# Weight rounding with two buffers per intermediate, a fourth staging place in two accumulators, and small softmax operations on POOL

## The chip, the cores and the metric

The kernel runs on one core of a Trainium2 chip. The time is the device time of one execution in microseconds; the median of three runs is 748.48 us (747.7 to 748.65). A core has five engines that work side by side and wait for one another by semaphores: TensorE (PE in the profile) multiplies matrices into PSUM, VectorE (DVE) and ScalarE (ACT) work on tiles in PSUM and SBUF, GpSimd (POOL) on tiles in SBUF alone, and SyncE (SP) issues the DMA transfers here. Each engine executes its own queue in order.

## The reference

Attention in both directions between 512 tokens and 32 state rows per head (4 batches, 8 heads, 64 features), then two pairs of dense layers over the 2176 resulting rows: 512 to 2048 with a leaky activation and back, and 512 to 2048 with softplus and back.

```
a = softmax(0.125 * x @ state^T);   xread = a @ state
a2 = softmax(0.125 * state @ x^T);  sread = a2 @ x
x = concat(xread, sread) per batch, heads side by side   # (2176, 512)
h = x @ w_in;  g = max(h, 0) + alpha * min(h, 0);  x = g @ w_out
h = x @ w2_in; g = max(h, 0) + log1p(exp(-abs(h)));  out = g @ w2_out
```

The weights come as 64-bit floats; x, state and the output are 32-bit.

## The kernel before

The work is cut into blocks of 512 columns: q counts the four quarters of the 2048 hidden features, b the four batches of 512 tokens, and b = 4 is a block of the 4 x 32 state rows. A matrix product is made of three matmuls (`mm3`, lines 140 to 142), because each operand is held as a high part and a low part of the remainder (`split`, lines 146 and 149).

**Weights.** There are 64 weight tiles of 128 x 512 64-bit numbers. Tile i is loaded by SP into one of three staging tiles `stg` (`wload`, line 192). `wconv` turns it into 32-bit numbers: ACT takes the exponent field from the top 16 bits into `exp` (L206) and rescales it into `top` (L207), DVE puts in the sign (L208), cuts out the exponent (L209) and multiplies the low 32 bits by it (L210), and POOL adds both parts (L211). There is one `top` and one `exp` tile. The result goes into its final place for the first layer's input weights (`is_whole`, tiles wi0h to wi3l), otherwise into one of four `cnv` tiles, from which `wprep` splits it into a high part (ACT) and a low part (POOL). `wconv` returns without work when it is as many tiles ahead of `wprep` as there are `cnv` tiles. At its end it calls `wload` for the next tile.

**Attention.** Eight groups i (a batch and one half of its heads) go through four steps: `at_scores` (s: scores on PE L273, copy on ACT L274, row maximum on DVE L275, L276 scales it, exponential on ACT L277, L278 adds a small number to the sum, reciprocal L279), `at_rows` (r: transposes L287, the softmax the other way, L290 to L296), `at_back` (b: transposes L303 and a split) and `at_read` (d: transposes L312, products L318, L328). Loads x (at_load_t, L254) and y (at_load_x, L258) bring a group's two forms of the tokens; y is first read in L318, x in L273. The scratch tiles of a group are taken from places that later hold accumulators or weights.

**State weights.** `sw_batch` (w, PE L242) multiplies the state of one batch by four whole weight tiles; block (q, b) of the first layer needs its result.

**Order.** The program text gives an order: the string LOADS (L is `wload`), then BEFORE, then the blocks, between the first of which the strings AMONG are called. In it p is `wprep` and c is `wconv`. The framework then sets the order of each engine's queue by a planned timeline of its own (`schedule_with_timeline_sim=True`), so that an instruction whose inputs the plan sees ready may pass earlier ones of the text; queues in the trace differ from the text accordingly. A block is `hidden` (PE, into one of four PSUM banks `pa`), `act` (ACT, DVE) and, three blocks later, `out_part` (PE, four banks `pb`), whose sums `out_take` gathers in the 17 accumulators acc0 to acc16.

Of the kernel before, what the change touches and what calls it, by code (L numbers as in the profile page):

```python
# [8 lines left out]
F32 = mybir.dt.float32  # L9
F32R = mybir.dt.float32r  # L10
BF16 = mybir.dt.bfloat16
U16 = mybir.dt.uint16
U32 = mybir.dt.uint32
I64 = mybir.dt.int64
AF = mybir.ActivationFunctionType
ALU = mybir.AluOpType
AX = mybir.AxisListType

P = 128
W = 512  # L20
# [5 lines left out]
SCALE = 0.125  # L26
# [16 lines left out]

LOADS = "L0 x0 L0 y0 x1 L0 x2 y2 y1"
BEFORE = "p0 s0 c0 s1 r0 p0 c0 r1 d0 b0 p0 x3 d1 y3 p0 w0 b1 p0 y4 s2 p0 r2 c0 x4 s3 w1 c0"
AMONG = ("d2 r3 b2", "d3 s4 x5", "b3", "r4", "s5 y5 p0 d4 x6", "p0 r5 s6", "y6 d5 r6 b4 b5", "", "y7 x7 s7 d6", "b6 r7", "d7 b7")

# [9 lines left out]
def mixer_kernel(  # L59
# [18 lines left out]
    def sbt(shape, dt, name):  # L78
        return sb.tile(shape, dt, tag=name, name=name)
# [6 lines left out]
    class Place:  # L86


        def __init__(self, name):
            self.name, self.t, self.dt = name, None, None  # L90
# [6 lines left out]
        f = property(lambda self: self.get(F32))  # L97
        r = property(lambda self: self.get(F32R))

    def sbp(name):  # L100
        return Place(name + "h"), Place(name + "l")

# [17 lines left out]
    stf = ex_p[0][0]  # L120
    wo_p = pairs(7, "wo")
    g_p = pairs(4, "g")
    acc = [Place(f"acc{i}") for i in range(17)]
    stg = [sbt([P, W], I64, f"stg{i}") for i in range(3)]
    cnv = [sbt([P, W], F32, f"cnv{i}") for i in range(4)]
    tmp = [sbt([P, W], F32, f"tmp{i}") for i in range(3)]
    top_t = [[sbt([P, W], BF16, f"{x}{i}") for i in range(1)] for x in ("top", "exp")]
    top_bias = sbt([P, 1], F32, "top_bias")
    ident = sbt([P, P], F32, "ident")
    alpha = sbt([P, DFF // P], F32, "alpha")  # L130
# [2 lines left out]
    st_n = [sbt([P, 2], F32, f"stn{i}") for i in range(3)]  # L133


    for x in acc + flat([sr] + wo_p + g_p + wi_p[:4] + at_p + sw_p + wi_p[4:] + ex_p):
        x.get(F32)

    def mm3(ps, lh, ll, rh, rl, start, stop):
# [45 lines left out]
    def is_whole(i):  # L185
        return wsrc[i][:2] == ("i", 0)

    def wload():
        i = nload[0]
        if i < len(wsrc):  # L190
            to, of = stg[i % len(stg)].bitcast(U16), wsrc[i][4].bitcast(U16)
            nc.sync.dma_start(out=to[:, 0 : 4 * W - 1], in_=of[:, 1 : 4 * W])
            nload[0] += 1

    def wconv():

        i = nconv[0]
        if i >= len(wsrc) or i >= nprep[0] + len(cnv):
            return
        s = stg[i % len(stg)]  # L200
        top = s.bitcast(U16).rearrange("p (n t) -> p n t", t=4)[:, :, 2]
        low = s.bitcast(U32).rearrange("p (n t) -> p n t", t=2)[:, :, 0]
        a = take_place(i).f if is_whole(i) else cnv[i % len(cnv)]
        t, e = (x[i % len(x)] for x in top_t)
        tu, eu = t.bitcast(U16), e.bitcast(U16)
        nc.scalar.activation(e, top.bitcast(BF16), AF.Abs)  # L206
        nc.scalar.activation(tu, eu, AF.Relu, bias=top_bias, scale=TOP_SCALE)  # L207
        nc.vector.scalar_tensor_tensor(out=tu, in0=top, scalar=TOP_SIGN, in1=tu, op0=ALU.bitwise_and, op1=ALU.bitwise_or)  # L208
        nc.vector.tensor_scalar(eu, tu, TOP_EXP, None, op0=ALU.bitwise_and)  # L209
        nc.vector.scalar_tensor_tensor(out=a, in0=low, scalar=REST, in1=e, op0=ALU.mult, op1=ALU.mult)  # L210
        nc.gpsimd.tensor_tensor(out=a, in0=t, in1=a, op=ALU.add)  # L211
        wload()
        nconv[0] += 1

    def wprep(n=1):
# [49 lines left out]
    def at_scores(i):  # L265

        b, g = i // 2, i % 2
        t, n2 = scratch(i), st_n[i % 3]
        ps = bank(pool_s(i))
        for k in range(2):  # L270
            for hh in range(2):
                r, o = slice(hh * D, (hh + 1) * D), col(g, k, hh)
                nc.tensor.matmul(ps[o : o + NS], stf.f[r, head(2 * g + k, b)], t[k][r], start=True, stop=True)  # L273
        nc.scalar.activation(t[4], ps, AF.Copy)  # L274
        nc.vector.tensor_reduce(out=n2[:, 0:1], in_=ps, op=ALU.max, axis=AX.X)  # L275
        nc.vector.tensor_scalar(n2[:, 0:1], n2[:, 0:1], -SCALE, None, op0=ALU.mult)  # L276
        nc.scalar.activation(t[5], ps, AF.Exp, bias=n2[:, 0:1], scale=SCALE, accum_out=n2[:, 1:2])  # L277
        nc.vector.tensor_scalar(n2[:, 1:2], n2[:, 1:2], EPS, None, op0=ALU.add)  # L278
        nc.vector.reciprocal(n2[:, 1:2], n2[:, 1:2])  # L279

    def at_rows(i):

        s0, e1 = scratch(i)[4], scratch(i)[1]
        m1, s1 = st_m[i % 2], st_s[i % 2]
        ps = bank(pool_s(i))
        for c in range(4):
            nc.tensor.transpose(ps[:, c * P : (c + 1) * P], s0[:, c * P : (c + 1) * P], ident)  # L287
        p3 = ps.rearrange("p (a n) -> p a n", n=NS)
        e3 = e1.rearrange("p (a n) -> p a n", n=NS)
        nc.vector.tensor_reduce(out=m1, in_=p3, op=ALU.max, axis=AX.X)  # L290
        nc.vector.tensor_tensor(out=e3, in0=p3, in1=m1.to_broadcast([P, 16, NS]), op=ALU.subtract)
        nc.scalar.activation(e1, e1, AF.Exp, scale=SCALE)
        nc.vector.tensor_reduce(out=s1, in_=e3, op=ALU.add, axis=AX.X)
        nc.vector.tensor_scalar(s1, s1, EPS, None, op0=ALU.add)
        nc.vector.reciprocal(s1, s1)
        nc.gpsimd.tensor_tensor(out=e3, in0=e3, in1=s1.to_broadcast([P, 16, NS]), op=ALU.mult)  # L296

# [260 lines left out]
```

## Time and profile before

| | |
|---|---|
| median of the runs | 748.48 us (747.7, 748.48, 748.65) |
| the profiled execution | 746.91 us, span 745.1 us |
| mean granted TensorE clock | 0.995 of full |
| busy, share of the span | PE 97%, DVE 57%, ACT 57%, POOL 23% |
| the chain that ended last, by engine | PE 95%, DVE 2%, ACT 1%, DMA 1% |
| DMA | 47.27 MB, mean 63 GB/s |

The profile is of one execution, whose own time stands beside its span: the 1.8 us between them lie outside the program's own instructions. Busy shares are means over stages that differ much: the first 40 us are loading, conversion and attention, the rest is mostly matmuls. A `<-` behind an idle time names what ended it. A line number names a line of the kernel before.

### The profile page before, as it was taken

Reading aid. Unit: us, or ns where it says so; the run is one execution under the profiler, and the core shown is the slowest. Engines: PE = TensorE matmul, PEld = TensorE weight load, DVE = VectorE, ACT = ScalarE, POOL = GpSimd, SP = SyncE. Lnnn points to the kernel's source line nnn. Section 1 sums busy time; section 2 is a strip of 40 time slices with the busy share of each in tenths; the row PEclk is TensorE's granted clock in tenths of the full one; section 3 lists DMA queues with packets and bytes.
Section 4 is the critical chain, followed back from the end, with each engine's and each line's share of the span. In section 5 each row is a group of like instructions: output and inputs, shape, how many; then the busy total and the mean of one; then the engine's idle time right before and its main releaser. Section 6 shows DMA issues by size and latency. Waiting matters only on the chain.

```text
span 745.1 us, 9504 instructions
## 1 busy us (share of the span) xinstructions
PE 722.4 (97%) x3580; PEld 561.6 (75%) x3580; DVE 425.2 (57%) x693; ACT 423.5 (57%) x764; POOL 170.8 (23%) x142
## 2 busy tenths in 40 slices
PE   5699998999999999999999999999999999999997
PEld 2267666777778777878888888888888888888886
DVE  4898657757778456886585224664257342333433
ACT  4778767735564235564677647765466454444560
POOL 2353332412142003462572004410044000000000
PEclk9989999999999999999999999999999999999999
DMA  9654313203211001220123001220010000001102
GB/s 320 224 177 154 104 41 128 86 1 113 85 57 57 0 1 49 93 85 1 40 74 113 0 1 45 97 86 0 1 53 5 1 1 0 1 1 56 57 15 113
DMA packets 16654, 47.27 MB, mean 63 GB/s; under 512 B 2016, under 2 KB 2016, under 8 KB 16608
## 3 DMA queue, kind: packets, MB, share of 16 engines
q1 hardware_dynamic: 16608, 46.66, 18.7%
q8 instruction: 28, 0.46, 0.3%
q14 instruction: 18, 0.15, 0.1%
HBM read 42.20 MB, written 4.46 MB: 63 GB/s over the span
## 4 chain that ended last, share of the span: by engine, by line
PE 95%; DVE 2%; ACT 1%; DMA 1%; issue 0%; POOL 0%; SPq 0%; ACTq 0%
PE pb L140 17%; PE pb L141 17%; PE pb L142 17%; PE pa L140 13%; PE pa L142 12%; PE pa L141 12%; PE pa L242 2%; PE pa L363 2%; PE pa L273 1%; DMA acc<-xt 1%; DVE top L208 1%; PE pa L371 0%; PE pa L312 0%; PE pb L273 0%; ACT exp L206 0%
## 5 line engine op out<-in xcount | busy, mean ns | idle before, releaser
L390 DVE SCALAR_TENSOR_TENSOR pa<-pa,tmp 128x512 f32<-128x512 f32 x68 | 47.4, 697 | 125.7 <-ACT tmp L389 125.7
L387 ACT ACTIVATE tmp<-pa 128x512 f32<-128x512 f32 x68 | 40.6, 597 | 89.2 <-PE pa L142 69.7
L433 DVE TENSOR_TENSOR acc<-pb,acc 128x512 f32<-128x512 f32 x102 | 67.4, 685 | 35.9 <-PE pb L142 35.9
L208 DVE SCALAR_TENSOR_TENSOR top<-stg,top 128x512 uint16<-128x512 uint16 x64 | 53.0, 828 | 47.5 <-ACT top L207 46.9
L211 POOL TENSOR_TENSOR cnv<-top,cnv 128x512 f32<-128x512 bf16 x48 | 56.3, 1174 | 100.6 <-DVE cnv L210 96.8
L383 DVE SCALAR_TENSOR_TENSOR pa<-tmp,rest,pa 128x512 f32<-128x512 f32 (+1 forms) x80 | 53.2, 671 | 25.5 <-ACT tmp L379 25.0
L206 ACT ACTIVATE exp<-stg 128x512 bf16<-128x512 bf16 x64 | 43.0, 672 | 39.6 <-DVE cnv L210 28.9
L379 ACT ACTIVATE tmp<-pa 128x512 f32<-128x512 f32 x68 | 40.2, 597 | 42.2 <-PE pa L142 35.7
L207 ACT ACTIVATE top<-exp,top_bias 128x512 uint16<-128x512 uint16 x64 | 46.2, 722 | 9.3 <-POOL cnv L211 5.7
L389 ACT ACTIVATE tmp<-tmp 128x512 f32<-128x512 f32 x68 | 42.9, 631 | 1.7
L388 ACT ACTIVATE tmp<-tmp 128x512 f32<-128x512 f32 x68 | 42.9, 631 | 1.5
L210 DVE SCALAR_TENSOR_TENSOR cnv<-stg,exp 128x512 f32<-128x512 uint32 x48 | 35.8, 745 | 12.8 <-POOL wo5l L149 4.0
L209 DVE TENSOR_SCALAR exp<-top 128x512 uint16<-128x512 uint16 x64 | 32.2, 503 | 1.1
L146 ACT ACTIVATE g1h<-pa 128x512 fp32r<-128x512 f32 x33 | 19.7, 597 | 20.5 <-DVE pa L390 12.3
L146 ACT ACTIVATE g3h<-pa 128x512 fp32r<-128x512 f32 x33 | 19.7, 597 | 19.4 <-DVE pa L383 9.7
L146 ACT ACTIVATE g0h<-pa 128x512 fp32r<-128x512 f32 x33 | 19.7, 596 | 19.1 <-DVE pa L383 10.2
L149 DVE TENSOR_TENSOR g3l<-pa,g3h 128x512 fp32r<-128x512 f32 x33 | 22.7, 689 | 13.5 <-ACT g3h L146 13.2
L149 DVE TENSOR_TENSOR g1l<-pa,g1h 128x512 fp32r<-128x512 f32 x33 | 22.7, 687 | 12.6 <-ACT g1h L146 12.2
L149 DVE TENSOR_TENSOR g0l<-pa,g0h 128x512 fp32r<-128x512 f32 x33 | 22.7, 688 | 10.5 <-ACT g0h L146 10.1
L149 DVE TENSOR_TENSOR g2l<-pa,g2h 128x512 fp32r<-128x512 f32 x33 | 22.7, 686 | 10.0 <-ACT g2h L146 9.9
L146 ACT ACTIVATE g2h<-pa 128x512 fp32r<-128x512 f32 x33 | 19.8, 599 | 14.5 <-DVE pa L390 7.6
L149 POOL TENSOR_TENSOR wo3l<-cnv,wo3h 128x512 fp32r<-128x512 f32 x5 | 6.5, 1304 | 74.5 <-ACT wo3h L146 74.3
(863 smaller groups left out, 2114.5 us busy)
## 6 DMA issues: line engine op xcount, KB each, us to landing
stg<-w1i SPq DMA_DIRECT2D x16, 511.8 KB, 4.1
stg<-w1o SPq DMA_DIRECT2D x16, 511.8 KB, 3.4
stg<-w2i SPq DMA_DIRECT2D x16, 511.8 KB, 4.0
stg<-w2o SPq DMA_DIRECT2D x16, 511.8 KB, 3.3
out<-acc SPq DMA_DIRECT2D x16, 256.0 KB, 2.0
acc<-xt SPq DMA_DIRECT2D x10, 256.0 KB, 4.5
acc<-xs SPq DMA_DIRECT2D x8, 256.0 KB, 5.1
wo4h<-xt SPq DMA_DIRECT2D x3, 256.0 KB, 3.8
```

Source lines behind the costliest of these rows:

```text
L140: nc.tensor.matmul(ps, lh, rh, start=start, stop=False)
L141: nc.tensor.matmul(ps, lh, rl, start=False, stop=False)
L142: nc.tensor.matmul(ps, ll, rh, start=False, stop=stop)
L146: nc.scalar.activation(h, src, AF.Copy)
L149: eng_l.tensor_tensor(out=l, in0=src, in1=h, op=ALU.subtract)
L206: nc.scalar.activation(e, top.bitcast(BF16), AF.Abs)
L207: nc.scalar.activation(tu, eu, AF.Relu, bias=top_bias, scale=TOP_SCALE)
L208: nc.vector.scalar_tensor_tensor(out=tu, in0=top, scalar=TOP_SIGN, in1=tu, op0=ALU.bitwise_and, op1=ALU.bitwise_or)
L211: nc.gpsimd.tensor_tensor(out=a, in0=t, in1=a, op=ALU.add)
L383: nc.vector.scalar_tensor_tensor(out=ps[:, cs], in0=t[:, cs], scalar=a, in1=ps[:, cs], op0=ALU.mult, op1=ALU.add)
L390: nc.vector.scalar_tensor_tensor(out=ps, in0=ps, scalar=0.0, in1=t, op0=ALU.max, op1=ALU.add)
L433: nc.vector.tensor_tensor(out=a, in0=ps, in1=a, op=ALU.add)
```

## The change

`top` and `exp` have two tiles each, used in turn. Of the four `cnv` tiles three remain. The accumulators acc0 and acc1 become the halves of one tile of twice the width; before they are used, the same memory is a fourth staging tile, for weight tile 3 alone, so LOADS issues four weight loads ahead of any conversion, and the conversion of tile 3 calls no `wload`. LOADS has another order: x1 and the third and fourth weights stand before y0. Three small operations of the softmax (128 x 1 twice, 128 x 16 once, per group) go from DVE to POOL.

```diff
-LOADS = "L0 x0 L0 y0 x1 L0 x2 y2 y1"
+LOADS = "L0 x0 L0 x1 L0 L0 y0 x2 y2 y1"
...
+    class Half:
+        def __init__(self, both, k):
+            self.name, self.both, self.k = f"{both['name']}{k}", both, k
+
+        @property
+        def f(self):
+            if "f" not in self.both:
+                self.both["f"] = sbt([P, 2 * W], F32, self.both["name"])
+            return self.both["f"][:, self.k * W : (self.k + 1) * W]
...
-    acc = [Place(f"acc{i}") for i in range(17)]
+    acc01 = {"name": "acc01"}
+    acc = [Half(acc01, 0), Half(acc01, 1)] + [Place(f"acc{i}") for i in range(2, 17)]
     stg = [sbt([P, W], I64, f"stg{i}") for i in range(3)]
-    cnv = [sbt([P, W], F32, f"cnv{i}") for i in range(4)]
+    stg_3 = sbt([P, W], I64, acc01["name"])
+    cnv = [sbt([P, W], F32, f"cnv{i}") for i in range(3)]
     tmp = [sbt([P, W], F32, f"tmp{i}") for i in range(3)]
-    top_t = [[sbt([P, W], BF16, f"{x}{i}") for i in range(1)] for x in ("top", "exp")]
+    top_t = [[sbt([P, W], BF16, f"{x}{i}") for i in range(2)] for x in ("top", "exp")]
...
-    for x in acc + flat([sr] + wo_p + g_p + wi_p[:4] + at_p + sw_p + wi_p[4:] + ex_p):
+    for x in acc[2:] + flat([sr] + wo_p + g_p + wi_p[:4] + at_p + sw_p + wi_p[4:] + ex_p):
...
+    def stage(i):
+        return stg_3 if i == 3 else stg[(i - (i > 3)) % len(stg)]
+
     def wload():
...
-            to, of = stg[i % len(stg)].bitcast(U16), wsrc[i][4].bitcast(U16)
+            to, of = stage(i).bitcast(U16), wsrc[i][4].bitcast(U16)
...
     def wconv():
...
-        s = stg[i % len(stg)]
+        s = stage(i)
...
-        wload()
+        if i != 3:
+            wload()
...
     def at_scores(i):
...
-        nc.vector.tensor_scalar(n2[:, 0:1], n2[:, 0:1], -SCALE, None, op0=ALU.mult)
+        nc.gpsimd.tensor_scalar(n2[:, 0:1], n2[:, 0:1], -SCALE, None, op0=ALU.mult)
         nc.scalar.activation(t[5], ps, AF.Exp, bias=n2[:, 0:1], scale=SCALE, accum_out=n2[:, 1:2])
-        nc.vector.tensor_scalar(n2[:, 1:2], n2[:, 1:2], EPS, None, op0=ALU.add)
+        nc.gpsimd.tensor_scalar(n2[:, 1:2], n2[:, 1:2], EPS, None, op0=ALU.add)
         nc.vector.reciprocal(n2[:, 1:2], n2[:, 1:2])
...
     def at_rows(i):
...
-        nc.vector.tensor_scalar(s1, s1, EPS, None, op0=ALU.add)
+        nc.gpsimd.tensor_scalar(s1, s1, EPS, None, op0=ALU.add)
         nc.vector.reciprocal(s1, s1)
```

## Rows read from the trace of the kernel before

**Rows 1.** The page: busy time and share of the span, TensorE

```profile
PE 722.4 (97%) x3580; PEld 561.6 (75%) x3580; DVE 425.2 (57%) x693; ACT 423.5 (57%) x764; POOL 170.8 (23%) x142
```

**Rows 2.** Stages: window, its length, busy time of each engine, clock, DMA share, GB/s

```profile
7.00:14.00 7.00, 6.01 (x19) 1.96 (x20) 4.88 (x12) 3.98 (x8) 1.16 (x1) 1.00 1.03 393
...
21.00:28.00 7.00, 5.51 (x63) 1.93 (x64) 4.37 (x10) 4.43 (x12) 2.27 (x3) 1.00 0.84 297
28.00:34.70 6.70, 3.44 (x28) 1.36 (x27) 6.23 (x14) 5.12 (x13) 2.43 (x2) 1.00 0.39 130
34.70:41.50 6.80, 6.09 (x50) 3.73 (x50) 6.68 (x15) 5.40 (x11) 3.90 (x3) 0.50 0.33 98
41.50:50.00 8.50, 8.50 (x78) 4.88 (x75) 8.43 (x17) 8.15 (x21) 4.99 (x4) 1.00 0.79 258
...
122.00:741.00 619.00, 619.00 (x2824) 498.17 (x2823) 334.72 (x511) 336.74 (x576) 129.85 (x102) 1.00 0.13 43
```

**Rows 3.** The list of waits of TensorE: total us, times, longest

```profile
PE pa L140 <- DVE g1l L149: 2.4, 1, 2.4
PE pa L312 <- ACT at7l L277: 1.9, 1, 1.9
...
PE pa L242 <- POOL wi1l L211: 1.4, 1, 1.4
```

**Rows 4.** Timeline of TensorE: start, duration, instruction, idle before it and its releaser

```profile
7.20 2.49 PE L273 MATMUL pb<-acc,ex0h 64*32 64x512 f32 x8 [7.20 <-DMA acc<-xt]
...
16.66 0.65 PE L318 MATMUL pa<-acc,acc 128*32 128x64 f32 x32
...
35.41 0.79 PE L140 MATMUL pa<-at0h,sw0h 128*128 128x512 f32 x1 [1.40 <-DVE stn L276]
```

**Rows 5.** The chain that ended last, 7 to 60 us: start, us

```profile
36.20 0.43 PE pa L141
...
42.28 0.23 PE pa L141
```

**Rows 6.** Timeline of ACT, 24 to 27 us

```profile
24.70 0.66 ACT L206 ACTIVATE exp<-stg 128x512 bf16<-128x512 bf16 x1 [1.56 <-DVE wi1l L210]
25.94 0.72 ACT L207 ACTIVATE top<-exp,top_bias 128x512 uint16<-128x512 uint16 x1 [0.58 <-POOL wi1l L211]
```

**Rows 7.** Timeline of DVE, 15 to 36 us

```profile
15.12 0.17 DVE L294 TENSOR_SCALAR sts<-sts 128x16 f32<-128x16 f32 x1
15.32 0.25 DVE L295 RECIPROCAL sts<-sts 128x16 f32<-128x16 f32 x1
...
16.78 0.15 DVE L276 TENSOR_SCALAR stn<-stn 128x1 f32<-128x1 f32 x1
16.86 0.68 DVE L290 TENSOR_REDUCE stm<-pa 128x16 f32<-128x512 f32 x1
...
21.85 1.29 DVE L208 SCALAR_TENSOR_TENSOR top<-stg,top 128x512 uint16<-128x512 uint16 x1 [0.47 <-ACT top L207]
...
26.70 0.69 DVE L208 SCALAR_TENSOR_TENSOR top<-stg,top 128x512 uint16<-128x512 uint16 x1 [2.03 <-ACT top L207]
27.42 0.29 DVE L209 TENSOR_SCALAR exp<-top 128x512 uint16<-128x512 uint16 x1
```

**Rows 8.** Timeline of POOL

```profile
21.55 1.05 POOL L296 TENSOR_TENSOR wo4l<-wo4l,sts 128x512 f32<-128x512 f32 x1 [0.49 <-DVE sts L295]
...
71.24 1.17 POOL L211 TENSOR_TENSOR wi3l<-top,wi3l 128x512 f32<-128x512 bf16 x1 [2.17 <-DVE wi3l L210]
```

**Rows 9.** DVE's groups by line, 7 to 60 us: busy, mean ns, idle before

```profile
L208 DVE SCALAR_TENSOR_TENSOR top<-stg,top 128x512 uint16<-128x512 uint16 x10 | 9.3, 934 | 9.8 <-ACT top L207 9.8
L209 DVE TENSOR_SCALAR exp<-top 128x512 uint16<-128x512 uint16 x10 | 4.6, 459 | 0.2
```

**Rows 10.** Timeline of SP's queue

```profile
13.27 0.33 SPq L192 DMA_DIRECT2D stg<-w1i  x1
```

**Rows 11.** The chain that ended last, whole span

```profile
104.47 1.02 PE pa L242 x16
```

## The prediction, made before the result was known

> **What bounds the kernel now.** I read the page's engine line first: TensorE is busy 722.4 us, 97% [rows 1]. The table by stage says where the other 3% lies: from 122 to 741 us TensorE is busy 619.00 of 619.00 us, so nothing that shortens another engine there can shorten the kernel; from 28 to 34.7 us it is busy 3.44 of 6.70 [rows 2]. The list of waits gives the pieces: 1.4 us until POOL finished the fourth rounded weight (wi1l), 1.9 us until ACT wrote an exponential into at7l, and a late one of 2.4 us (behind DVE's g1l) [rows 3]. The timeline adds 1.40 us in front of the first matmul of the first `hidden` block, which starts at 35.41 [rows 4]. Its named releaser is the tiny L276, but in DVE's order the subtraction sw2l, which frees a PSUM bank, ended just before; I take it as a wait for DVE as a whole. From 35.41 on the chain that ends last is nearly all TensorE. One more loss is no gap: in 34.7 to 41.5 the granted clock is 0.50, the 1.2 GHz level, with TensorE busy 6.09 us [rows 2], and a matmul of the chain takes 0.43 us there, 0.23 after it [rows 5].
>
> So only the head (7 to 41 us) and that late stall can change. DVE is what the head runs on: 6.68 of 6.80 us in the slow-clock stage and 8.43 of 8.50 in the next, but only 4.37 of 7.00 in 21 to 28 [rows 2]. It idles there because the rounding of a weight has one `top` and one `exp` tile: ACT's L206 of the next weight sat 1.56 us until DVE's L210 had read `exp`, its L207 then 0.58 us until POOL's L211 had read `top` [rows 6], and DVE sat 2.03 us for that L207, and 0.47 us for the one before [rows 7].
>
> **The change, part by part.**
>
> Two `top` and two `exp` tiles. L206 and L207 of a weight no longer wait for L210 and L211 of the one before. This takes the two DVE waits, 2.03 + 0.47 = 2.50 us. What is late next is the data: see the loads. Bounds: nothing (the order within ACT and DVE leaves the same holes), and 4.7 us (the three waits of TensorE 1.4 + 1.9 + 1.40 all go). I take 2.50, the row of the wait itself.
>
> A price comes with it. DVE's L208 at 21.85 took 1.29 us while POOL's L296 ran from 21.55 to 22.60 [rows 7, 8]. It ended 0.54 us after POOL did: it was held. In 7 to 60 us the ten L208 average 934 ns and the ten L209 459 [rows 9], against 0.69 and 0.29 where POOL is idle (26.70 and 27.42) [rows 7]: 0.24 + 0.17 = 0.41 us per weight is lost already. In the kernel before, L208 of a weight can never meet L211 of the weight before, since L207 waits for that L211; with two tiles it can. Bounds: nothing more, and a whole L211 more, 1.17 us [rows 8]. I take half of today's loss, 0.2, for each of the four weights that stand before the first `hidden`: +0.8.
> The Trainium skill (GPSIMD Engine Reference, 8. Key points) states that GpSimd shares its SBUF interfaces with VectorE and that they contend when a DVE instruction runs in a 2-port mode or has two SBUF inputs; the held L208 agrees. By that rule alone one would leave the new tiny POOL operations out of POOL, and take the loss nearer to its upper bound.
>
> Tiny operations to POOL: L276, L278, L294, eight of each. On DVE an L276 holds its queue 0.08 us (start 16.78, the next 16.86), an L294 0.20 (15.12 to 15.32) [rows 7]. Before 35.4 us there are four L276, three L278, two L294: 7 x 0.08 + 2 x 0.20 = 1.0 us off DVE. The trace has no such operation on POOL. From below, its latency is as on DVE, no loss; from above it starts behind a whole L211, 1.17 us. Behind it wait ACT's exponential L277 (for L276) and DVE's reciprocal L295 (for L294), and with them all that is queued on ACT and DVE; L278's reader, the reciprocal L279, is wanted much later. I take 0.15, the DVE duration once more as the price of the detour, since POOL is about half free (4.99 busy of 8.50 at its fullest [rows 2]); on L276 and L294 of the first two groups, which stand on the way to the first `hidden`: +0.6.
> The Trainium skill (the same page, 4.1 Engine selection) sends elementwise work to VectorE and calls GPSIMD about twice slower on two inputs; no run here shows it for one input and 16 columns, and doubling an L294 would add 0.17 each time, so the sum would hardly move.
>
> Loads. The fourth weight was issued at 13.27 [rows 10], after the first had been converted; now it goes out with the first loads, and the second activation group's x1 goes before y0. At 393 GB/s (7 to 14 us, DMA share 1.03 [rows 2]) half a megabyte is 1.3 us. y0 moves behind x1 and two weights, 4.0 us; x2, y2, y1 and the alpha vector move 1.3 us. x0's first half starts TensorE at 7.20; behind it come its other half, three weights, x1 and y0, 2.8 MB in all, so y0 is there by 14.5. Its first reader, L318, starts at 16.66 [rows 4]: 2 us of cover, cost nothing; without that cover the d0 step would slip, up to 4 us. The fourth weight is there at about 13. That is what lets the second buffer work; no term of its own. The next load waits for no conversion that it did not wait for before.
>
> Fourth staging place. It lies in acc0 and acc1, which are first written by the first block's `out_take`, and that comes behind the first `hidden` (35.41 [rows 4]), while conversion 3 must be over before that `hidden` can start. Nothing; a wait there would hold one ACT copy.
>
> Three `cnv` instead of four. `wconv` stops three ahead of `wprep`. Counting the calls, conversions from the tenth on move back by one call, and conversion 11 (wi3l) goes from block 5 of the first quarter to block 10, right before the `sw_batch` that reads it. In the trace it ran at 71.24 [rows 8] and that batch at 104.47 [rows 11], 33 us later: the planner runs conversions far ahead of the text, and that hides the move. Nothing. Without that cover one conversion is open, 0.7 + 0.7 + 0.7 + 0.3 + 0.7 + 1.2 = 4.3 us.
>
> Clock. What TensorE did before the clock fell was 3.44 us of work in 6.70, with the three gaps above; behind the 5.51 in 7.00 of the stretch ahead of it no fall came [rows 2]. With 2.1 us (2.5 + 1.0 - 0.8 - 0.6) less idle in front of 35.4 the first becomes more like the second; from what share of work on the clock stays up no row tells. If the fall goes, 6.09 x (1 - 0.23/0.43) = 2.8 us are won [rows 2, 5]. Below nothing is possible too: another hole may bring a fall elsewhere. I take half, -1.4.
>
> The late stall of 2.4 us [rows 3] sits behind ACT and DVE queues full of block work; I leave it, bounds 0 to 2.4 won.
>
> Sum: -2.5 + 0.8 - 1.0 + 0.6 - 1.4 = -3.5 us. The profiled execution took 746.91 us (span 745.1), which gives 743.4 for such a one; it lay 1.6 us under the median of the runs, 748.48, and I forecast the median: 745.0.
>
> **The rivals.**
> Better: all three head gaps close and the clock stays up: 4.7 + 2.8 = 7.5, 741.0. For it: DVE has 2.6 us idle in 21 to 28 to give. Against it: behind 35 us DVE has nearly none [rows 2], and an earlier `hidden` only asks more of it.
> No change: DVE, full from 28 us on, gives the earlier start back by 50 us, or the planner's order keeps the holes; the change then doesn't do what it says. 748.
> Slower: DVE held by POOL. With L207 freed, L208 comes straight after L210 of the weight before and waits out its L211. A weight then loses 1.17 instead of 0.41; over the eight weights of the head 8 x 0.76 = 6.1 us on the engine that bounds it, against 2.5 + 1.0 won and 0.6 lost: +3.2, clock as now, 751.7. It decides from (2.5 + 1.0 - 0.6) / 8 = 0.36 us more per weight. For it: the held L208; against it: DVE has other work to place between.
>
> **How the numbers follow.** Forecast 0.47 (its own range 743 to 747), better 0.17, no change 0.20, slower 0.16. 0.2% is 1.5 us, about what can be told from no change. Faster: 0.45 of the forecast and the better case, 0.62; same 0.22; slower 0.16. The range takes in most of the better case and the near part of the slower one: 740 to 750.5.
>
> **What would show it.** Right: the 2.03 us wait of L208 for L207 is gone; the first `hidden` matmul starts at 33 us or earlier; L207 no longer follows L211; the granted clock between 28 and 42 us is 1.00 throughout. Wrong: L208 or L209 means over 1.2 and 0.8 us in the head (the lock); DVE or ACT idle behind L294 or L276 on POOL for over 0.5 us; new TensorE waits for y0 in front of 18 us, or at the `sw_batch` near 104 us; the stretch from 122 us no longer full. The prediction fails if the first `hidden` starts earlier and the end does not.

## The result, and the profile after

The kernel after takes 752.74 us (752.3 to 753.2), the kernel before on the same chip 748.18: a ratio of 1.0061 [1.0044, 1.0078], 4.6 us slower. The forecast of 745.0 had the wrong sign. The experiments below split the 4.6 us into parts of both signs, most of them larger than it.

The profiled execution has a span of 751.4 us against 745.1, 6.3 us more. That is 1.7 us more than the medians differ by, because the two profiled executions are not the middle ones: the one of before took 746.91 us, below its median, the one of after 753.20, above its own. TensorE's busy time and its gaps account for it: busy 724.7 against 722.4 [rows 1], +2.3, which leaves +4.0 of idle time. The page of the kernel after, with the groups of the rounding (L225, L226 and L227 are the L208, L209 and L210 of before, L228 is L211; L224 is L207):

```profile
PE 724.7 (96%) x3580; PEld 563.2 (75%) x3580; DVE 438.6 (58%) x669; ACT 422.6 (56%) x764; POOL 183.9 (24%) x166
...
L228 POOL TENSOR_TENSOR cnv<-top,cnv 128x512 f32<-128x512 bf16 x48 | 60.2, 1255 | 58.8 <-DVE cnv L227 58.6
...
L225 DVE SCALAR_TENSOR_TENSOR top<-stg,top 128x512 uint16<-128x512 uint16 x63 | 57.6, 915 | 17.2 <-ACT top L224 16.8
...
L226 DVE TENSOR_SCALAR exp<-top 128x512 uint16<-128x512 uint16 x64 | 36.7, 573 | 1.2
```

DVE runs 24 instructions fewer than before (669 against 693) and is busy 13.4 us more (438.6 against 425.2 [rows 1]). An L225 that nothing holds takes 0.69 us, an L226 0.29 [rows 7]; the means here are 0.915 and 0.573. The stages of [rows 2] in the kernel after, with one more, 108 to 124 us:

```profile
21.00:28.00 7.00, 5.58 (x43) 1.40 (x39) 6.56 (x12) 4.04 (x8) 3.96 (x4) 1.00 0.78 283
28.00:34.70 6.70, 3.61 (x28) 1.57 (x28) 6.65 (x10) 5.58 (x15) 5.45 (x7) 0.98 0.65 200
34.70:41.50 6.80, 5.61 (x47) 3.60 (x50) 6.77 (x12) 5.00 (x11) 4.01 (x6) 0.51 0.55 166
41.50:50.00 8.50, 7.13 (x72) 4.34 (x65) 8.34 (x13) 7.51 (x20) 7.04 (x7) 1.00 0.63 212
108.00:124.00 16.00, 11.60 (x58) 7.35 (x56) 13.73 (x25) 11.64 (x21) 6.32 (x5) 0.98 0.61 187
122.00:741.00 619.00, 616.09 (x2798) 495.12 (x2799) 344.43 (x510) 335.75 (x576) 130.16 (x101) 0.99 0.13 41
```

The two tiles do what they are for: DVE is busy 6.56 us in 21 to 28 instead of 4.37, though 1.7 us of that are two instructions held by POOL (an L225 of 1.52 us and an L226 of 1.14). Taken with the rest of the change, TensorE gets next to nothing from it: 5.58 against 5.51 and 3.61 against 3.44; the slow-clock stage is still there; the stage behind it, full before, lacks 1.37 us; and the stretch from 122 us is no longer full. Before, TensorE was busy 13.60 us in 108 to 124, DVE 11.56 and POOL 4.04:

```profile
108.00:124.00 16.00, 13.60 (x66) 8.93 (x66) 11.56 (x22) 10.74 (x20) 4.04 (x4) 1.00 0.30 99
```

The place is one stall. It was 2.4 us [rows 3]; in TensorE's list of waits after (total, times, longest) it is the 5.1:

```profile
PE pa L154 <- DVE sw2l L163: 6.3, 2, 5.1
```

In TensorE's timeline it ends at 124.67, and the first `hidden` starts at 36.08 instead of 35.41 [rows 4]:

```profile
36.08 0.80 PE L154 MATMUL pa<-at0h,sw0h 128*128 128x512 f32 x1 [1.19 <-DVE sw2l L163]
...
124.67 0.80 PE L154 MATMUL pa<-at6h,sw6h 128*128 128x512 f32 x1 [5.07 <-DVE sw2l L163]
```

In the last part of that stall the granted clock falls to 0.50 (the 1.2 GHz level) a second time, which it did not do there before:

```profile
123.30:130.00 6.70, 5.33 (x13) 4.22 (x14) 5.67 (x12) 3.72 (x7) 1.17 (x1) 0.50 0.19 57
```

Added up: the gaps ahead of the first `hidden` and with it 15.0 us instead of 15.3, -0.3; gaps in 36 to 51 us +1.75; the late stall +2.67; others -0.1; and +2.3 of busy time, for which the second low-clock stretch is enough (5.33 us x (1 - 0.23/0.43) = 2.5 [rows 5]): 6.3.

### The profile page after: what moved, and what is told of

Its sections match the earlier page's. It is cut to its first block, busy times and chain, and to the rows that moved or that the text cites. A ratio compares the mean times of both kernels' runs of the same rounds, so it can differ in the third digit from the quotient of the medians.

```text
span 751.4 us, 9484 instructions
## 1 busy us (share of the span) xinstructions
PE 724.7 (96%) x3580; PEld 563.2 (75%) x3580; DVE 438.6 (58%) x669; ACT 422.6 (56%) x764; POOL 183.9 (24%) x166
## 4 chain that ended last, share of the span: by engine, by line
PE 88%; DVE 4%; DMA 3%; ACT 2%; POOL 1%; issue 1%; SPq 1%; POOLq 0%; ACTq 0%; DVEq 0%
PE pb L154 16%; PE pb L155 16%; PE pb L156 16%; PE pa L154 12%; PE pa L156 12%; PE pa L155 12%; PE pa L260 2%; PE pa L381 1%; DVE top L225 1%; DMA acc<-w1i 1%; DVE cnv L227 1%; DMA wo5l<-xs 1%; DMA stg<-w1o 1%; DVE exp L226 1%; DMA stg<-w1i 1%
## 5 line engine op out<-in xcount | busy, mean ns | idle before, releaser
L228 POOL TENSOR_TENSOR cnv<-top,cnv 128x512 f32<-128x512 bf16 x48 | 60.2, 1255 | 58.8 <-DVE cnv L227 58.6
L401 DVE SCALAR_TENSOR_TENSOR pa<-tmp,rest,pa 128x512 f32<-128x512 f32 (+1 forms) x80 | 53.2, 670 | 31.9 <-ACT tmp L397 31.6
L225 DVE SCALAR_TENSOR_TENSOR top<-stg,top 128x512 uint16<-128x512 uint16 x63 | 57.6, 915 | 17.2 <-ACT top L224 16.8
L397 ACT ACTIVATE tmp<-pa 128x512 f32<-128x512 f32 x68 | 40.1, 596 | 44.9 <-PE pa L156 38.4
L227 DVE SCALAR_TENSOR_TENSOR cnv<-stg,exp 128x512 f32<-128x512 uint32 x48 | 41.7, 870 | 15.3 <-POOL wo5l L163 4.0
L224 ACT ACTIVATE top<-exp,top_bias 128x512 uint16<-128x512 uint16 x64 | 46.0, 719 | 6.7 <-POOL cnv L228 4.2
L226 DVE TENSOR_SCALAR exp<-top 128x512 uint16<-128x512 uint16 x64 | 36.7, 573 | 1.2
L163 DVE TENSOR_TENSOR g3l<-pa,g3h 128x512 fp32r<-128x512 f32 x33 | 22.7, 689 | 15.3 <-ACT g3h L160 15.1
L163 DVE TENSOR_TENSOR g2l<-pa,g2h 128x512 fp32r<-128x512 f32 x33 | 22.7, 687 | 13.4 <-ACT g2h L160 13.4
```

What stands on the lines that cost most here:

```text
L163: eng_l.tensor_tensor(out=l, in0=src, in1=h, op=ALU.subtract)
L401: nc.vector.scalar_tensor_tensor(out=ps[:, cs], in0=t[:, cs], scalar=a, in1=ps[:, cs], op0=ALU.mult, op1=ALU.add)
```

## The experiments

"Late stall" is TensorE's gap near 119 us (2.40 before, 5.07 after). Ratios are to the kernel before on the same chip.

| kernel | ratio [95%] | late stall |
|---|---|---|
| before, tiny operations on POOL (e18) | 0.9910 [0.9896, 0.9924] | 2.38 |
| before, three `cnv` (e1) | 0.9986 [0.9977, 0.9995] | 2.33 |
| + tiny on POOL (e16) | 0.9921 [0.9908, 0.9934] | 1.64 |
| + tiny on POOL, two `exp` (e15) | 0.9944 [0.9931, 0.9956] | 1.71 |
| + two `top`, two `exp` (e6) | 1.0091 [1.0077, 1.0105] | 5.75 |
| after | 1.0061 [1.0044, 1.0078] | 5.07 |
| single `top`, `exp` (e4) | 0.9985 [0.9976, 0.9994] | 1.52 |
| single, tiny on DVE (e11) | 1.0004 [0.9996, 1.0013] | 2.32 |
| two `exp` only (e9) | 0.9967 [0.9955, 0.9978] | 1.81 |
| two `top` only (e10) | 0.9969 [0.9957, 0.9981] | 1.71 |
| both double for four weights (e5) | 0.9974 [0.9965, 0.9983] | 1.53 |
| e5, tiny on DVE (e12) | 1.0000 [0.9991, 1.0010] | 2.3 |
| two `exp`, two `top` for four weights (e14) | 0.9997 [0.9989, 1.0006] | 2.33 |
| tiny on DVE (e3) | 1.0159 [1.0145, 1.0173] | 5.75 |
| fourth `cnv` (e2) | 1.0090 [1.0076, 1.0104] | 4.78 |
| fourth staging tile (e7) | 1.0103 [1.0087, 1.0118] | 5.27 |
| five short adds (e13) | 1.0078 [1.0065, 1.0091] | 4.78 |
| e7 and e13 together (e17) | 1.0038 [1.0024, 1.0052] | 2.40 |

A "+" is on top of e1; the rows from e4 on are the kernel after with that edit.

Where a part acts can be read from TensorE's idle time, added up from the lists of gaps in the traces (us; "head" is all idle time up to the start of the first `hidden`):

| kernel | head | first `hidden` at | behind it, to 60 | late stall |
|---|---|---|---|---|
| before | 15.3 | 35.41 | 0.0 | 2.40 |
| tiny on POOL (e18) | 11.4 | 31.43 | 0.9 | 2.38 |
| three `cnv` (e1) | 15.2 | 35.21 | 0.0 | 2.33 |
| + tiny on POOL (e16) | 12.6 | 30.88 | 0.9 | 1.64 |
| + two `top`, two `exp` (e6) | 13.4 | 33.43 | 2.6 | 5.75 |
| after with single tiles (e4) | 17.5 | 37.09 | 0.0 | 1.52 |
| after | 15.0 | 36.08 | 1.6 | 5.07 |

**Is it the three `cnv`?** (e1, e2) In the kernel after, ACT waits for a load near 109 us; the first theory was that three `cnv` tiles, by holding conversions back, send the loads late. e1 takes one `cnv` tile from the kernel before; e2 gives the kernel after a fourth, in memory that is used later (`cnv_of(i)` in place of `cnv[i % len(cnv)]` for i < 24).

```diff
-    cnv = [sbt([P, W], F32, f"cnv{i}") for i in range(4)]
+    cnv = [sbt([P, W], F32, f"cnv{i}") for i in range(3)]
```

> The kernel before with three cnv tiles in place of four, nothing else. Theory A (late loads): conversion 15 must wait until the split of weight 12 has read its cnv tile (POOL's L149 of wo4l, 106 us), so the loads of weights 18 and 19 go out 14 us later than before and ACT stands in front of them; the stall of 2.4 us near 119 us grows to about 5 us and the clock falls behind it: 751 to 754. Theory B (lock: DVE held by POOL in the head): nothing of it is here, 748.2 within 0.5.

> The changed kernel with a fourth cnv tile for weights 0 to 23 (it lies in wi5h, which is not used before the second pair of layers). Theory A: loads of weights 16 to 18 go out before 95 us again, the stall near 119 us is back to about 2.4 us with no fall of the clock behind it: 747 to 749. Theory B: 751.5 to 753, since the head is as in the changed kernel.

Neither fits: e1 is faster than before by 0.14%, e2 no faster than after. The theory falls.

**The tiny operations and the second tiles** (e3, e4). e3 puts the three operations back on DVE in the kernel after, e4 takes its second `top` and `exp` away.

```diff
-        nc.gpsimd.tensor_scalar(n2[:, 0:1], n2[:, 0:1], -SCALE, None, op0=ALU.mult)
+        nc.vector.tensor_scalar(n2[:, 0:1], n2[:, 0:1], -SCALE, None, op0=ALU.mult)
...
-    top_t = [[sbt([P, W], BF16, f"{x}{i}") for i in range(2)] for x in ("top", "exp")]
+    top_t = [[sbt([P, W], BF16, f"{x}{i}") for i in range(1)] for x in ("top", "exp")]
```

> The changed kernel with L276, L278 and L294 back on DVE. Theory A: the late stall stays, 751.5 to 753. Theory C (the tiny operations' detour and their share of the lock are the loss): the gaps of 1.8 us between 44 and 51 us go and the first hidden starts before 35 us: 748 to 749.5.

> The changed kernel with one top and one exp tile, as before. Theory A: the late stall stays about 5 us, 751.5 to 753. Theory B (conversions meet POOL more often with two buffers, DVE is held): the mean of L225 and L226 in 7 to 60 us falls under that of the changed kernel (957 and 480 ns) and the time to 748 to 749.

The loss is the second tiles: without them 0.9985 and a late stall of 1.52. The tiny operations are not to blame; without their move the kernel is another 1% slower.

**Where do the second tiles lose?** (e5, e6)

```diff
-        t, e = (x[i % len(x)] for x in top_t)
+        t, e = (x[i % 2 if i < 4 else 0] for x in top_t)
```

> The changed kernel with two top and two exp tiles for weights 0 to 3 alone; from weight 4 on one of each. Theory B (two buffers bunch the conversions: DVE is held by POOL more often, and the bunches stand in ACT's and DVE's queues ahead of block work): nearly all the loss comes from weight 4 on, the stall near 119 us is 1.5 to 2.5 us again, the gaps of 1.8 us between 44 and 51 us go, 745 to 747.5. Theory E (it is the first four weights, whose early conversion takes ACT and DVE from the softmax of the first groups): 751 to 753.

> The kernel before with three cnv tiles and two top and exp tiles; tiny operations on DVE, three staging tiles, loads as before. Three cnv tiles alone took 746.0. Theory B: two buffers alone cost what they cost in the changed kernel: 752 to 759, stall near 119 us over 4 us, DVE held 4 us or more between 60 and 160 us (0.3 without them). Theory F (they cost only together with the early loads): 746 to 748.

e6 is the kernel before with three `cnv` and both second tiles: the loss comes alone, with its stall. e5, which is double for the first four weights only, loses nothing: the price is paid by the weights behind the fourth. The head by itself does win. Beside the rest of the change the second tiles take 2.5 us of TensorE's idle time out of it (17.5 in e4, 15.0 in the kernel after), without the rest 1.8 (15.2 in e1, 13.4 in e6). The first `hidden` of e4, and then that of e6, which has no gap in front of it and takes 0.50 us instead of 0.79:

```profile
37.09 0.79 PE L154 MATMUL pa<-at0h,sw0h 128*128 128x512 f32 x1 [1.62 <-DVE sw2l L163]
```

```profile
33.43 0.50 PE L140 MATMUL pa<-at0h,sw0h 128*128 128x512 f32 x1
```

All of it is given back behind that `hidden`: 1.6 and 2.6 us in new gaps before 60 us, where e4 and e1 have none, and 3.55 and 3.42 us in the late stall.

**Is ACT standing before loads the cause?** (e7) A fourth staging tile for the weights 4 to 31, in memory used later; each load goes out one conversion sooner.

```diff
-        return stg_3 if i == 3 else stg[(i - (i > 3)) % len(stg)]
+        if i == 3:
+            return stg_3
+        if i < 4 or i >= 32:
+            return stg[(i - 32) % 3 if i >= 32 else i]
+        return (stg + [stg_w])[i % 4]
```

> The changed kernel with a fourth staging tile for weights 4 to 31 as well (in the pair wi5, not used before the second layers), so that each load goes out one conversion earlier. Theory G (ACT stands in front of loads that have not landed, 3.9 us of it between 108 and 117 us): the stall of 5.1 us falls to 2 us or less and no clock fall follows, 747 to 749. Theory B in its form of lock and order: the stall stays over 4 us, 751 to 753.

No: ACT's waits for loads at 110 and 114 us are gone, and the stall is 5.27.

**What does POOL do to DVE?** (e8) A kernel without the computation: the kernel's DVE operations alone, and again beside twelve adds like L228 on POOL.

```diff
+    for k in range(2):
+        last = round_of(k)          # eight DVE operations, POOL idle
+    for _ in range(12):
+        nc.gpsimd.tensor_tensor(out=gc, in0=top, in1=ga, op=ALU.add)
+    for k in range(2):
+        last = round_of(k + 2)      # the same eight, beside the twelve adds
```

> No part of the computation: eight DVE operations of the kernel's shapes twice alone, then twice beside a row of twelve POOL additions like L211 (1.17 us each). Lock theory: the 16-bit forms of L208 and L209 and the form of L210 (both inputs in SBUF) end only behind a POOL operation, 1.2 us or more each, and so does a TENSOR_TENSOR with both inputs in SBUF; a TENSOR_TENSOR with one input in PSUM and a reduction keep their 0.68 us. No lock: all keep the durations they have alone, within 10%.

Its DVE timeline, first alone, then beside POOL (L50 to L52 are the L225 to L227, L54 has two inputs in SBUF, L57 is the tiny 128 x 16):

```profile
9.07 0.29 DVE L51 TENSOR_SCALAR ob<-top 128x512 uint16<-128x512 uint16 x1
...
10.48 0.68 DVE L54 TENSOR_TENSOR oe<-fa,fb 128x512 f32<-128x512 f32 x1
...
11.73 0.16 DVE L57 TENSOR_SCALAR oh<-sm 128x16 f32<-128x16 f32 x1
...
12.70 1.26 DVE L51 TENSOR_SCALAR ob<-top 128x512 uint16<-128x512 uint16 x1
13.88 0.68 DVE L52 SCALAR_TENSOR_TENSOR oc<-stg,exp 128x512 f32<-128x512 uint32 x1
14.48 0.68 DVE L53 TENSOR_TENSOR od<-ps,fa 128x512 f32<-128x512 f32 x1
15.08 1.04 DVE L54 TENSOR_TENSOR oe<-fa,fb 128x512 f32<-128x512 f32 x1
...
16.70 0.47 DVE L57 TENSOR_SCALAR oh<-sm 128x16 f32<-128x16 f32 x1
```

DVE's last operation beside the adds is this one, and it ends at 22.15:

```profile
21.68 0.47 DVE L57 TENSOR_SCALAR oh<-sm 128x16 f32<-128x16 f32 x1
```

POOL's rows, the twelve adds in one and one alone:

```profile
12.65 16.89 POOL L67 TENSOR_TENSOR gc<-top,ga 128x512 f32<-128x512 bf16 x12
...
29.81 0.22 POOL L74 TENSOR_SCALAR gb<-col 128x1 f32<-128x1 f32 x1
30.11 1.16 POOL L76 TENSOR_TENSOR gc<-top,gb 128x512 f32<-128x512 bf16 x1
```

L51 takes 1.26 instead of 0.29, L54 1.04 instead of 0.68, L57 0.47 instead of 0.16. L53, with an input in PSUM, is not held, nor are a reduction (0.67) and the 128 x 1 (0.14), nor is L52 here, right behind an operation that has just been held. POOL pays too: 16.89 / 12 = 1.41 us per add against 1.16, as a mean. DVE works beside the adds for the first 9.5 us only; if the other 7.4 us hold adds of 1.16, 6.4 of them, the 5.6 beside DVE took 1.7 each, an estimate. In the kernel after, the L228 at 118.30, beside an L225 of DVE, takes 1.66. The Trainium skill (GPSIMD Engine Reference, 8. Key points) names two kinds of DVE instructions that contend with GpSimd, those in a 2-port mode and those with two SBUF inputs; the probe agrees for L54, which has two inputs in SBUF. L51 and L57 have one input, and no row names their mode: that they are held fits that sentence only if they run in a 2-port mode.

**One tile or both?** (e9, e10)

```diff
-        t, e = (x[i % len(x)] for x in top_t)
+        t, e = top_t[0][0], top_t[1][i % 2]
```

> The changed kernel with two exp tiles and one top tile, for all weights: L223 of the next weight may run early, but its L224 waits until L228 of the weight before has read top, so its L225 can't meet that L228. Theory B, lock: DVE is held about 1 us between 60 and 160 us in place of 4.8, the stall near 119 us is under 2.5 us, 745.5 to 748. Theory H (early conversions take ACT's and DVE's queues, lock or no lock): conversions still follow each other faster than with one tile of each, 749 to 753.

> The changed kernel with two top tiles and one exp tile: L223 of the next weight waits for L227 of the one before; L224 and L225 then come some 1.4 us behind it, when L228 (1.2 us) is over or nearly so. Theory B, lock: little hold, 745.5 to 748. Theory H: as the changed kernel or a little faster, 749 to 753.

e10 has the second `top` and one `exp`. Either tile alone loses nothing and is 0.9% better than both. With one of them single, a conversion still waits for a step of the one before, and the conversions stay apart: in e9 POOL's adds start at 104.3, 109.1, 113.0, 117.5 and 123.5 us; in the kernel after at 106.4, 110.1, 112.3, 115.2, 118.3 and 120.9.

**The loads, and the tiny operations in other company** (e11, e12). e11 is e4 with the tiny operations on DVE, e12 the same edit to e5.

> The changed kernel without both the second top and exp tiles and the move of the tiny operations: the fourth staging place, the order of the loads and three cnv tiles remain. Three cnv tiles alone took 746.0, all but the second tiles 746.2. If loads and tiny operations each do nothing: 746 to 746.4. If one of them gains what the other loses: 744.5 or 748.

> The kernel with two top and exp tiles for weights 0 to 3 alone (745.9), with the tiny operations back on DVE. If their move to POOL takes work off a full DVE in the head: 747 to 748.5. If it is worth nothing once the conversions are spaced: 745.5 to 746.3.

The tiny operations win 0.19% (e11 to e4) and 0.26% (e12 to e5) here. e11 is 0.18% slower than e1: the loads and the fourth staging place do not come free.

**Holding or order?** (e13, e17) In e13, on the kernel after, the adds of five weights take 16 of their 512 columns, and the rest of that sum is left out; the order of the queues stays but for single steps.

```diff
-        nc.gpsimd.tensor_tensor(out=a, in0=t, in1=a, op=ALU.add)
+        n = 16 if 16 <= i <= 20 else W
+        nc.gpsimd.tensor_tensor(out=a[:, :n], in0=t[:, :n], in1=a[:, :n], op=ALU.add)
```

> The changed kernel, with POOL's add of the weights 16 to 20 cut to 16 of its 512 columns: the rest of that sum is left out, so the low parts of these five weights stand alone in 496 columns. Those five adds then last some 0.3 us instead of 1.2, and nothing else of the kernel is taken out. Theory H (the loss is DVE held by POOL): the holds of L225 and L226 in 108 to 124 us, some 3 us, go, and the late stall of 5.07 us shrinks to 1.5 to 2.5; the second stretch at the 0.50 clock goes with it; 749.5 us or less (3 us under the changed kernel). Theory O (the loss is the order: conversions bunch ahead of the state block's work on ACT and DVE, whoever holds what): the bunch stays, the stall stays over 4 us, 751.5 or more. Between: both have a share.

DVE is held no more in 108 to 124 us, and the stall is 4.78: theory H, as put, falls. But e13 still has the load waits, and e7 had the holding. e17 is e7 with the edit of e13:

> The staging of e7 (a fourth place for the weights 4 to 31, so ACT stands before no load near 115 us) and the short adds of e13 (POOL adds 16 of 512 columns for the weights 16 to 20, the rest of that sum left out) in one kernel; the order of the changed kernel stays. e7 took the loads' wait away and kept the stall (5.27, DVE held 3.5), e13 took the holding away and kept the stall (4.78, ACT idle 2.39 for a load). Theory O (ACT's queue has four more of the rounding's steps ahead of the two L397 that the stall waits for): with neither wait left the two L397 still come behind them, at 119 or later against a state block's transposes at 117.2, and the stall is 3 to 4.5 us. Theory J (either of two waits is enough, order alone costs nothing): it falls to 2 or less, and the time to 749 or less.

The stall is 2.40, between the two expectations and nearer to J: with this order of the queues either of the two waits is enough for the long stall, and with neither it lies 0.9 us above e4's 1.52. The chain can be read in ACT's queue. Behind two L397 of ACT (the first step of a block's activation, before DVE's L401) come its sw2h and DVE's sw2l (the high and the low part of a state weight, read out of a PSUM bank), which ends the stall. In the kernel after:

```profile
110.45 0.67 ACT L223 ACTIVATE exp<-stg 128x512 bf16<-128x512 bf16 x1 [1.41 <-DMA stg<-w1i]
...
114.89 0.67 ACT L223 ACTIVATE exp<-stg 128x512 bf16<-128x512 bf16 x1 [2.19 <-DMA stg<-w1i]
115.65 0.72 ACT L224 ACTIVATE top<-exp,top_bias 128x512 uint16<-128x512 uint16 x1
116.72 0.68 ACT L223 ACTIVATE exp<-stg 128x512 bf16<-128x512 bf16 x1 [0.34 <-DMA stg<-w1o]
117.48 0.72 ACT L224 ACTIVATE top<-exp,top_bias 128x512 uint16<-128x512 uint16 x1
118.11 1.55 ACT L449 ACTIVATE acc<-pb 128x512 f32<-128x512 f32 x3
119.63 0.66 ACT L223 ACTIVATE exp<-stg 128x512 bf16<-128x512 bf16 x1
120.19 0.58 ACT L449 ACTIVATE acc<-pb 128x512 f32<-128x512 f32 x1
120.67 0.59 ACT L397 ACTIVATE tmp<-pa 128x512 f32<-128x512 f32 x1
```

Three weights' steps stand in front of L397 in the queue, and the first of them is late; L397 comes 4.1 us behind the transposes of the state block, which TensorE starts at 116.58. In e9 the steps of one weight stand there, late by a wait of the same kind, and L397 comes 1.7 us behind the transposes (114.15):

```profile
113.21 0.67 ACT L223 ACTIVATE exp<-stg 128x512 bf16<-128x512 bf16 x1 [2.16 <-DMA stg<-w1i]
...
114.74 0.72 ACT L224 ACTIVATE top<-exp,top_bias 128x512 uint16<-128x512 uint16 x1
...
115.83 1.09 ACT L397 ACTIVATE tmp<-pa 128x512 f32<-128x512 f32 x2
```

In e7, where the loads are there, the same rounding steps are late because DVE is held: five operations there, of which these are two (L243 is its L225, L244 its L226), lose 0.52 + 0.59 + 0.86 + 0.86 + 0.67 = 3.5 us against 0.29 and 0.69:

```profile
113.22 1.28 DVE L243 SCALAR_TENSOR_TENSOR top<-stg,top 128x512 uint16<-128x512 uint16 x1
...
116.27 1.15 DVE L244 TENSOR_SCALAR exp<-top 128x512 uint16<-128x512 uint16 x1
```

In e17, with neither, ACT's L397 (L416 there) starts at 118.45:

```profile
118.45 0.61 ACT L416 ACTIVATE tmp<-pa 128x512 f32<-128x512 f32 x1
```

e17 is still 0.38% slower than before: in its head TensorE has a gap of 3.60 us (behind ACT's wi4l), and the clock is at 0.50 in two stretches there. That part of the loss lies in the head, and no run takes it apart.

**What were the other parts worth?** (e14, e15, e16, e18) e14 is the two winners put together:

```diff
-        t, e = (x[i % len(x)] for x in top_t)
+        t, e = top_t[0][i % 2 if i < 4 else 0], top_t[1][i % 2]
```

> The changed kernel with two exp tiles throughout and the second top tile for the first four weights alone: the two best versions so far (745.86 and 745.22) put together. If what each wins is its own (the head's from both tiles, the spacing later from one top tile): 744.5 or less. If both take away the same loss and no more: 745.2 to 745.9.

0.9997, which neither reading expected: together they win nothing. The last three build on the kernel before, with its loads and staging: e18 moves the tiny operations and nothing else, e16 has three `cnv` as well, e15 two `exp` tiles on top of that.

```diff
-        nc.vector.tensor_scalar(s1, s1, EPS, None, op0=ALU.add)
+        nc.gpsimd.tensor_scalar(s1, s1, EPS, None, op0=ALU.add)
...
-    top_t = [[sbt([P, W], BF16, f"{x}{i}") for i in range(1)] for x in ("top", "exp")]
+    top_t = [[sbt([P, W], BF16, f"{x}{i}") for i in range(n)] for x, n in (("top", 1), ("exp", 2))]
```

> The kernel before with three cnv tiles, the tiny operations on POOL and two exp tiles, one top; the order of the loads and the staging as before. It asks what the fourth staging place and the loads' order are worth beside one doubled tile: if something, it is slower than the 745.22 of the changed kernel with two exp and one top, by up to 1.5 us (746.7); if nothing or less (three cnv alone gave 746.02, with the loads 747.77), 744 to 745.2.

> The kernel before with three cnv tiles and the tiny operations on POOL, single top and exp tiles, loads and staging as before. Three cnv alone took 746.02. If the tiny operations on POOL win by themselves what they won beside the new loads (1.6 us): 744.4. If their gain was only to mend what the new loads had cost: 746 or more.

> The kernel before with the tiny operations on POOL and nothing else; four cnv tiles. With three cnv it took 741.63 (e16), three cnv without the tiny move 746.02 (e1), so the tiny move is worth 4.4 there, and three cnv 1.4 by themselves. If both are worth the same apart: 747.3 - 4.4 = 742.9. If the tiny move needs three cnv: 745 to 747.

All three are faster than expected. The tiny operations win 0.65% beside three `cnv` (e1 to e16) and 0.9% without; the second `exp` tile, which costs nothing beside the new loads, costs 0.2% here; whether three `cnv` cost anything beside the tiny operations the intervals of e16 and e18 leave open. The new loads and the fourth staging place lose in every pair: 0.18% (e1 to e11), 0.64% (e16 to e4), 0.23% (e15 to e9).

e18 is the best kernel of all: 740.4 us, 0.9910 of before, 1.5% faster than the kernel after. Two stages, first of the kernel before:

```profile
28.00:35.00 7.00, 3.44 (x28) 1.36 (x27) 6.53 (x14) 5.33 (x14) 2.60 (x3) 0.98 0.37 124
35.00:42.00 7.00, 6.59 (x51) 3.96 (x52) 6.88 (x15) 5.38 (x12) 3.88 (x4) 0.54 0.39 123
```

and of e18, where TensorE has work and the clock stays up:

```profile
28.00:35.00 7.00, 6.24 (x67) 3.61 (x60) 6.72 (x12) 5.82 (x11) 4.10 (x5) 1.00 0.40 143
35.00:42.00 7.00, 6.85 (x70) 4.12 (x70) 6.86 (x13) 6.96 (x21) 5.07 (x7) 1.00 0.86 273
```

Its first `hidden` starts at 31.43, 4.0 us sooner than before, with a matmul of 0.48 us where it was 0.79 [rows 4]:

```profile
31.43 0.48 PE L140 MATMUL pa<-at0h,sw0h 128*128 128x512 f32 x1
```

In DVE's timeline the subtraction sw2l, which frees a PSUM bank ahead of that `hidden`, starts at 27.70; before it started at 34.68:

```profile
27.70 0.67 DVE L149 TENSOR_TENSOR sw2l<-pa,sw2h 128x512 fp32r<-128x512 f32 x1
```

The move took 1.0 us of work off DVE ahead of 35 us, by the forecast's count. The rest goes with another order: without the tiny operations in DVE's queue the framework puts the block work elsewhere among the softmax. TensorE's transposes of the third group stand behind the wait for wi1l [rows 3] in the kernel before, and ahead of that weight's products in e18 (before, then e18):

```profile
27.80 0.66 PE L287 MATMUL pa<-ident,wi4l 128*128 128x128 f32 x4
```

```profile
24.33 0.66 PE L287 MATMUL pa<-ident,wi4l 128*128 128x128 f32 x4
```

No run keeps the order and moves the operations, so that the order makes the rest of the gain is read from these rows and not shown by itself. Why the framework orders as it does no trace shows.

## Why the prediction was wrong, step by step

The runs give the parts in one order, at 748.18 us (ratio steps times that): tiny operations -6.7 (e18), three `cnv` +0.8 (e16, not told from zero), loads and fourth staging place +4.8 (e4), second tiles +5.7 (after). Sum +4.6, the measured change, as it must be for steps that build on one another. In other orders a part has other sizes: three `cnv` -1.0 alone (e1), the tiny operations -1.4 (e11 to e4) to -7.3 (e3 to after), the loads and staging +1.3 (e1 to e11), the second tiles +7.9 (e1 to e6).

**Two tiles, -2.5 + 0.8: the step that failed.** The wait it priced went as forecast: no gap of DVE's L225 at 26 us. In 7 to 60 us DVE waits 6.6 us for L224 instead of 9.8 [rows 9], but nearly all of the 6.6, and 7.01 of the 9.8, lie ahead of the first such instruction, which stands for the first weight; so of 2.8 us behind it nothing is left. TensorE's idle time in the head fell with it, by 2.5 us beside the rest and by 1.8 without, near the 1.7 of the sum. But the step "what is late next is the data: see the loads" looked at the head alone. The rounding goes on behind the head, and there the freed steps of ACT stand in its queue ahead of a block's L397. I gave the late stall "bounds 0 to 2.4 won", with no loss below, because both queues were "full of block work"; that was the reason to ask for more. The late stall grew by 2.67 us over before and by 3.55 over e4, the gaps between the first `hidden` and 60 us by 1.6 over e4, and the second low-clock stretch came on top.

**The holding, 0.2 for four weights.** The size was right without the rest of the change and too small with it. The means of 7 to 60 us hardly move:

```profile
L225 DVE SCALAR_TENSOR_TENSOR top<-stg,top 128x512 uint16<-128x512 uint16 x13 | 12.4, 957 | 6.7 <-ACT top L224 6.6
L226 DVE TENSOR_SCALAR exp<-top 128x512 uint16<-128x512 uint16 x13 | 6.2, 480 | 0.1
```

That is 0.02 + 0.02 = 0.04 us more per weight than in [rows 9], plus three L227 of 1.18 to 1.37 us instead of 0.69, 1.7 us in all. But ahead of 35.4 us, where the forecast put its price, DVE's timeline has eight L225 instead of six, and what the rounding's steps take there beyond 0.69, 0.29 and 0.69 us is 4.2 us instead of 1.1: +3.1, where the sum had +0.8. It counted the four weights that the first `hidden` needs; the freed steps bring later ones ahead of it as well. In e6 the same count is 2.1 against 1.1 in e1. The rival "slower" named the right engine pair and a near number (751.7). It wanted 0.76 more per weight in the head; 4.2 us on eight weights against 1.1 on six is 0.35 more, just under its threshold of 0.36. So it was nearer than the means say, but its path was another: it had the time lost in the head, where the second tiles gained. The holding is also one of the two waits in 108 to 124 us, which it did not look at.

**Tiny operations, -1.0 + 0.6.** The sign is right, the size 6.7 instead of 0.4. The work moved was counted, the order that follows was not: TensorE's idle time in the head fell by 4.0 us (15.3 to 11.4, e18), and the slow-clock stage went. The detour's price, +0.15 per use, was low where DVE is busy. In the kernel after, POOL's timeline has tiny operations of 0.22 us, and one of 0.66 beside DVE's L225 of 15.27 to 15.95; in 7 to 60 us ACT idles behind L294 only twice, 0.35 and 0.93 us (L294 and L296 here are the L276 and L278 of before):

```profile
15.37 0.66 POOL L294 TENSOR_SCALAR stn<-stn 128x1 f32<-128x1 f32 x1
...
16.92 0.22 POOL L296 TENSOR_SCALAR stn<-stn 128x1 f32<-128x1 f32 x1 [0.54 <-DVE exp L226]
```

**Loads and fourth staging place, nothing: the second step that failed.** The fourth weight landed at 12.6, y0 by 13.9, as worked out, and y0 held nobody, the first d0 product waiting for ACT:

```profile
15.44 0.65 PE L336 MATMUL pa<-acc,acc 128*32 128x64 f32 x32 [0.85 <-ACT acc L331]
```

Yet the pair costs 4.8 us beside the tiny operations (e16 to e4): the first `hidden` goes from 30.88 to 37.09 us, and TensorE's idle time in the head from 12.6 to 17.5. In e4 neither ACT nor DVE waits for a load in 22 to 38 us; ACT's and DVE's queues have another order: DVE's row maximum of the third group starts at 28.30 in e4 and at 23.89 in e16. TensorE waits for a load anew only in the kernel after, 0.99 us for the tokens x3 at 25.29. So what failed is the reasoning that a load which holds nobody costs nothing. Which of the two edits brings it was not tried apart, and why the order changes stays open.

**Three `cnv`, nothing.** The forecast holds within about 1 us: -1.0 alone (e1), +0.8 beside the tiny operations, not told from zero.

**Clock, -1.4.** Wrong sign, +2.3. "Another hole may bring a fall elsewhere" was in the text as a bound of nothing; a hole that the change itself widens was not.

Of the signs named ahead, the 2.03 us wait is gone; the first `hidden` at 33 us or earlier, and the clock at 1.00 in 28 to 42, did not come with the whole change, but both came with e18, which leaves out the rest. Of the signs of being wrong, two came: ACT idle 0.93 us behind the moved L276, and the stretch from 122 us no longer full. And e6 is the case in which the prediction was to fail: its first `hidden` starts 1.8 us sooner than in e1, and its end comes 1.05% later.

## What to carry to other kernels

A second buffer takes away a wait and with it a spacing: before adding it, look in every stage where the loop runs, not only where the wait was, at what the freed steps will stand in front of in an in-order queue, and give that a loss in the bounds. A mean over a longer window can hide a price: count how many operations moved into the stage as well. Where a framework orders the queues, an edit of a few tenths of a microsecond can move the end by ten times that, either way, so try each part alone before they are joined: here one part of the change was worth 7 us and the others gave all of it back and more. Two waits that each suffice hide one another; take both away before either is cleared.

## What the runs showed of the hardware

POOL and DVE hold each other: in e8 a DVE operation goes from 0.29 to 1.26 us beside adds of 1.16, another from 0.16 to 0.47; an add of POOL takes 1.66 beside DVE in the kernel after, and a tiny one 0.66 instead of 0.22. A DVE operation right behind a held one ran at its own length (e8: 0.68).

The length of TensorE's late gap does not say by itself whether the clock falls: behind gaps of 1.64 (e16) and 2.33 us (e14) it fell to 0.50, behind 2.40 (before), 2.38 (e18) and 2.40 us (e17) it stayed at 1.00. The two low stretches, e16 and then e14:

```profile
116.40:119.80 3.40, 3.40 (x10) 2.62 (x9) 2.63 (x5) 1.97 (x4) 1.17 (x1) 0.50 0.45 157
```

```profile
120.90:124.30 3.40, 3.24 (x8) 2.56 (x9) 2.50 (x5) 1.13 (x3) 1.17 (x1) 0.50 0.45 148
```
